# Weights in two and three pieces in place of four, and a new order of every queue, in an attention and feed-forward kernel

## The chip, the cores and the metric

The kernel runs on one core of one Trainium2 chip. The metric is the device time of one execution in microseconds; the time given is the median of three runs. The profile is of one more execution, taken by the hardware profiler.

## The reference

Linear attention over 8 batches and 8 heads (576 tokens, 64 dimensions), then a feed-forward part over the 4,608 tokens with 512 channels:

```
q_s = softmax(q, axis=-1);  k_s = softmax(k, axis=2)      # exp of (x - max), over its sum + 1e-9
kv  = einsum('bhsd,bhse->bhde', k_s, v)
x   = einsum('bhsd,bhde->bhse', q_s, kv)  ->  [4608, 512]
out = ((x @ w1) * (x @ w2)) @ w3 @ w_out                  # w1, w2: 512x1024; w3: 1024x1024; w_out: 1024x512
```

All inputs and the output are float32.

## The kernel before

Matrix work is done in fp16. w3 @ w_out is folded once into W3O (1024x512), so that each token needs two products up (with w2 and w1), an elementwise product, and one product down.

The tokens are worked in nine chunks of 512: chunk b (0 to 7) holds the first 512 tokens of batch b, and chunk 8 the last 64 of all eight. Chunks 0 and 1 are worked as two halves of 256 tokens (`sub` 0 and 1, four steps `u` each); the others as one piece (eight steps).

Every piece of work is a named step, and one list, ORDER, gives the order of all steps. Each engine runs its steps in the order of the list, so the list sets the order of every queue; what a step waits for follows from its data and its buffers. A suffix /A, /D or /P puts a step on ScalarE, VectorE or GpSimd. A step that uses the data path which VectorE and GpSimd share is linked to the one before it on the other engine. The steps, with the letters used below:

- loads: `w3.r` (a block of 128 rows of w3), `wo.h` (half of w_out), `w1.i` and `w2.i` (pieces by columns), `k.b`, `q.b`, `v.b` (a batch; some as two pieces, `k.0.0`, `q.1.1`). GpSimd issues those of the weights and of batches 0 and 1 (it casts the weights to fp16 on the way, line 302); SyncE issues q.0 at the start and all loads from batch 2 on. SyncE's first load after q.0 (`q.2`) is made to wait for the third-last load of GpSimd (GATE = 3).
- fold: `w3t.f` transposes a block of w3 on TensorE (L334), `w3T.f` evicts it (two buffers), `pf.f.0` and `pf.f.1` multiply it by w_out (L344), `W3O.f` evicts the result. `zero.i` are matmuls on zeros (L251), which fill TensorE's waits in the start; ZEROS gives 13 for `zero.0`, and for the others ORDER gives the count.
- attention of batch b: `kmx` (L375, L382), `cb` (the maximum over the tokens, spread to all partitions), `ksub` (L414), `kexp`; `qmx` (L477), `qsub` (L483), `qexp`, `qsm` (the sum, L509), `qeps`, `qrc`, `qn` (L527); `vc` (a cast of v, L220); `kv` on TensorE (L440), `kv2` divides by the sums (L458 to L461); `qd` transposes q by DMA (L561, on SyncE), for batch 0 `qt` and `qT` on TensorE and an eviction; `xm` and `xt` multiply q by kv (L579: the first 512 tokens and the last 64), `xs` and `xts` evict them (L224, L226).
- chunk c: `up.1.c.sub.u` multiplies by w2 and `up.0.c.sub.u` by w1 (L723, each into one PSUM bank of 512), `bs` evicts the first as fp16 (L220), `ab` multiplies the two (VectorE, L738), `down.c.t` multiplies 128 tokens by W3O (L745, L760 for the last chunk), `os` evicts them (L220), `st` stores them (SyncE).

TensorE writes into eight PSUM banks, taken in turn: a step waits until the bank taken eight places earlier has been evicted. GpSimd's loads have eight semaphores, also taken in turn, so that a load is issued only when the one eight places earlier has landed.

A step of `up` needs the piece of w1 or w2 that holds its columns; the piece is found from COLS:

```
COLS = [(0, 256), (256, 512), (512, 768), (768, 1024)]
ws = lambda n, u: [(n, [i for i, (a, b) in enumerate(COLS) if a < (u + 1) * nf * P <= b][0])]
```

Of the kernel before, what the change touches and what calls it, by code (L numbers as in the profile page):

```python
# [64 lines left out]
zero.6/1 zero.3/1 q.0.0 qmx.0.0 qsub.0.0/D q.0.1 qmx.0.1 ident w3.7 qexp.0.0 qsm.0.0 zero.1/6 zero.5/1 zero.0  # L65
w3.4 w3t.4 w3T.4/A qsub.0.1/D qexp.0.1 qeps.0.0/D qrc.0.0 qn.0.0/D w3t.7 w3T.7/A wo.0 zero.2/6 pf.4.0 qt.0.0.4
pf.7.0 qsm.0.1 qeps.0.1/D qrc.0.1 qt.0.0.0 w3.6 w3t.6 wo.1 pf.4.1 k.0.0 qn.0.1/D qT.0.0.4/A kmx.0.0 w3T.6/A
pf.7.1 W3O.7/A qT.0.0.0/A W3O.4/A k.0.1 kmx.0.1 cb.0 ksub.0.0/D qt.0.1.4 qt.0.1.0 pf.6.0 zero.4/1 w3.5 w3t.5
qT.0.1.0/A qT.0.1.4/A w3T.5/A pf.6.1 W3O.6/A w3.0 w3t.0 pf.5.0 pf.5.1 w3.3 w3T.0/A pf.0.0 w3t.3 pf.0.1 W3O.5/A
kexp.0.0 w3.2 w3t.2 w3.1 w3t.1 v.0 q.1.0 w2.3 w3T.3/D pf.3.0 pf.3.1 w3T.1/A ksub.0.1/D kexp.0.1 k.1 W3O.0/A  # L70
kv.0.0 qmx.1.0 kv.0 kv2.0 pf.1.0 pf.1.1 w2.2 w2.1 w3T.2/A W3O.3/A qsub.1.0/D xm.0.1 xm.0.0 xs.0.0.0/D
xs.0.1.0/D w1.2 q.1.1 w1.3 kmx.1.0 cb.1 pf.2.0 pf.2.1 w1.1 w2.0 w1.0 v.1 W3O.1/A xs.0.0.1/A up.1.0.0.3
xs.0.1.1/A qexp.1.0 up.1.0.1.3 up.1.0.1.2 bs.0.1.2/D qmx.1.1 ksub.1.0/P bs.0.0.3/A up.1.0.0.2 bs.0.1.3/A
up.1.0.0.1 up.1.0.1.1 bs.0.0.2/A W3O.2/A bs.0.0.1/A up.0.0.1.2 up.0.0.0.2 qsm.1.0 up.0.0.0.3 ab.0.0.3
bs.0.1.1/D ab.0.1.2 up.0.0.1.3 up.0.0.0.1 ab.0.1.3 ab.0.0.2 up.1.0.0.0 bs.0.0.0/D qeps.1.0/A qrc.1.0 ab.0.0.1
up.1.0.1.0 up.0.0.1.0 bs.0.1.0/A ab.0.1.0 qsub.1.1/P up.0.0.0.0 ab.0.0.0 qexp.1.1 qsm.1.1 kexp.1.0 up.0.0.1.1
ab.0.1.1 qeps.1.1/A qrc.1.1 ksub.1.1/P qn.1.0/P q.2 qmx.2.0 qmx.2.1 down.0.0 os.0.0/A kexp.1.1 down.0.1
os.0.1/A vc.1.0/P vc.1.1/P kv.1.0 kv.1 kv2.1 down.0.2 os.0.2/A k.2 kmx.2.0 kmx.2.1 xt.0 qd.1.0 xm.1.0 cb.2
qn.1.1/P down.0.3 st.0.0 xts.0.1/A qsub.2.0/P xs.1.0.0/A xts.0.0/A xs.1.0.1/A up.1.1.0.0 os.0.3/A up.0.1.0.0
up.1.1.0.1 bs.1.0.0/A ab.1.0.0 qd.1.1 qsub.2.1/P qexp.2.1 ksub.2.0/P qexp.2.0 qsm.2.0 xm.1.1 up.0.1.0.1  # L80
up.1.1.0.2 bs.1.0.1/A ab.1.0.1 xs.1.1.1/A up.0.1.0.2 up.1.1.0.3 xs.1.1.0/A kexp.2.0 qsm.2.1 qeps.2.0/A qrc.2.0
bs.1.0.3/A bs.1.0.2/A q.3 qmx.3.0 ksub.2.1/P qn.2.0/P up.0.1.0.3 ab.1.0.3 ab.1.0.2 up.1.1.1.0 up.0.1.1.0
up.1.1.1.1 bs.1.1.1/A qeps.2.1/A up.0.1.1.1 up.1.1.1.2 up.0.1.1.2 bs.1.1.0/A bs.1.1.2/A up.1.1.1.3 down.1.0
up.0.1.1.3 k.3 kmx.3.1 qrc.2.1 ab.1.1.1 qmx.3.1 ab.1.1.2 ab.1.1.0 v.2 q.4 qmx.4.1 vc.2.0/A qsub.3.0/P qexp.3.0
kexp.2.1 qd.2.0 qn.2.1/P st.0.1 down.1.1 os.1.0/A bs.1.1.3/A vc.2.1/P kv.2 os.1.1/A qsub.3.1/P qexp.3.1
ab.1.1.3 qsm.3.0 qeps.3.0/A down.1.2 os.1.2/A qd.2.1 kv2.2 xm.2.1 qsm.3.1 xs.2.1.1/A xm.2.0 xs.2.0.1/A xt.1
kmx.3.0 xs.2.0.0/A xs.2.1.0/A qsub.4.1/P down.1.3 qeps.3.1/A qrc.3.1 qn.3.1/P cb.3 ksub.3.1/P ksub.3.0/P
xts.1.1/A qexp.4.1 os.1.3/A xts.1.0/A qsm.4.1 qeps.4.1/A k.4 kmx.4.0 up.1.2.0.0 bs.2.0.0/A up.0.2.0.0
up.1.2.0.1 up.0.2.0.1 up.1.2.0.2 up.0.2.0.2 up.1.2.0.3 bs.2.0.2/A bs.2.0.1/A ab.2.0.0 ab.2.0.2 ab.2.0.1
qrc.4.1 qrc.3.0 up.0.2.0.3 bs.2.0.3/A ab.2.0.3 up.1.2.0.4 bs.2.0.4/A up.0.2.0.4 up.1.2.0.5 kexp.3.1 ab.2.0.4  # L90
qmx.4.0 up.0.2.0.5 up.1.2.0.6 v.3 st.1.1 q.5 up.0.2.0.6 up.1.2.0.7 up.0.2.0.7 vc.3.1/A bs.2.0.5/A kexp.3.0
bs.2.0.6/A vc.3.0/A kmx.4.1 ab.2.0.5 v.4 st.0.2 ab.2.0.6 qn.3.0/P st.1.2 qd.3.1 st.0.3 vc.4.1/P qn.4.1/P
qsub.4.0/P kv.3 bs.2.0.7/A ab.2.0.7 down.2.0 kv2.3 xt.2 xts.2.0/A os.2.0/A qd.3.0 cb.4 qmx.5.1 xm.3.1 xm.3.0
xs.3.0.1/D down.2.1 xts.2.1/A xs.3.1.1/A xs.3.1.0/A qexp.4.0 qsm.4.0 k.5 kmx.5.1 st.1.0 v.5 down.2.2 down.2.3
q.6 vc.4.0/A xs.3.0.0/A qeps.4.0/A qrc.4.0 os.2.1/A os.2.3/A up.1.3.0.0 up.0.3.0.0 bs.3.0.0/D qmx.5.0 ab.3.0.0
ksub.4.1/P kmx.5.0 cb.5 qsub.5.1/P qd.4.1 st.1.3 v.6 st.2.1 qn.4.0/P ksub.4.0/P up.1.3.0.1 up.0.3.0.1 os.2.2/A
bs.3.0.1/A qexp.5.1 kexp.4.1 up.1.3.0.2 up.0.3.0.2 up.1.3.0.3 up.0.3.0.3 up.1.3.0.4 up.0.3.0.4 bs.3.0.2/A
ab.3.0.1 ab.3.0.2 st.2.3 kexp.4.0 bs.3.0.3/A bs.3.0.4/A up.1.3.0.5 up.0.3.0.5 st.2.2 qsub.5.0/P ksub.5.1/P
vc.5.1/P up.1.3.0.6 up.0.3.0.6 up.1.3.0.7 ab.3.0.3 qsm.5.1 qmx.6.0 st.2.0 qd.4.0 ab.3.0.4 qexp.5.0 bs.3.0.6/A
bs.3.0.5/A ab.3.0.5 ab.3.0.6 kv.4 kv2.4 up.0.3.0.7 bs.3.0.7/A ab.3.0.7 qeps.5.1/A qsm.5.0 qeps.5.0/A down.3.0  # L100
os.3.0/A vc.5.0/A xm.4.0 xm.4.1 xt.3 down.3.1 down.3.2 xts.3.0/D qrc.5.0 xs.4.0.1/D qrc.5.1 qmx.6.1 ksub.5.0/P
qsub.6.0/P k.6 kmx.6.1 kmx.6.0 qsub.6.1/P xs.4.1.0/A os.3.1/A xs.4.0.0/A xs.4.1.1/A up.1.4.0.0 xts.3.1/D
vc.6.0/A down.3.3 qexp.6.0 qsm.6.0 os.3.3/A q.7 qmx.7.0 qn.5.1/P qn.5.0/P cb.6 ksub.6.0/P qsub.7.0/P kexp.5.1
kexp.5.0 os.3.2/A qd.5.0 k.7 st.3.1 qd.5.1 bs.4.0.0/A up.0.4.0.0 up.1.4.0.1 ab.4.0.0 v.7 bs.4.0.1/D up.0.4.0.1
up.1.4.0.2 up.0.4.0.2 bs.4.0.2/A qexp.6.1 up.1.4.0.3 up.0.4.0.3 bs.4.0.3/A up.1.4.0.4 up.0.4.0.4 ab.4.0.2
ab.4.0.1 qmx.7.1 ab.4.0.3 up.1.4.0.5 up.0.4.0.5 up.1.4.0.6 up.0.4.0.6 bs.4.0.6/D kv.5 bs.4.0.4/A kexp.6.0
bs.4.0.5/A ab.4.0.4 ab.4.0.5 ab.4.0.6 up.1.4.0.7 qeps.6.0/A qexp.7.0 qsm.7.0 up.0.4.0.7 bs.4.0.7/A ab.4.0.7
down.4.0 down.4.1 ksub.6.1/P kexp.6.1 st.3.3 st.3.0 qsm.6.1 kv2.5 qeps.7.0/A qrc.7.0 qeps.6.1/A qrc.6.1
os.4.1/D st.4.1 xt.4 qrc.6.0 xts.4.1/D os.4.0/A xts.4.0/A qsub.7.1/P qexp.7.1 vc.6.1/P kv.6 kv2.6 xm.5.1
qn.6.1/P xm.5.0 xs.5.0.1/A vc.7.1/A xs.5.0.0/A xs.5.1.1/A kmx.7.1 qsm.7.1 qeps.7.1/D st.3.2 down.4.2 down.4.3  # L110
os.4.3/D xs.5.1.0/A up.1.5.0.0 bs.5.0.0/A up.0.5.0.0 kmx.7.0 up.1.5.0.1 bs.5.0.1/A os.4.2/A up.0.5.0.1
up.1.5.0.2 up.0.5.0.2 up.1.5.0.3 ab.5.0.1 ab.5.0.0 qrc.7.1 up.0.5.0.3 up.1.5.0.4 up.0.5.0.4 up.1.5.0.5
up.0.5.0.5 qn.7.1/P bs.5.0.3/A bs.5.0.4/A cb.7 bs.5.0.2/D qn.6.0/D ab.5.0.2 ab.5.0.3 vc.7.0/P ksub.7.1/P
bs.5.0.5/A up.1.5.0.6 ab.5.0.4 bs.5.0.6/A up.0.5.0.6 ab.5.0.6 up.1.5.0.7 bs.5.0.7/A ab.5.0.5 qd.6.1 up.0.5.0.7
st.4.0 qd.6.0 st.4.2 ksub.7.0/D xm.6.0 xm.6.1 xt.5 qd.7.1 xs.6.0.1/A xs.6.0.0/A ab.5.0.7 down.5.0 down.5.1
os.5.1/D xs.6.1.1/D down.5.2 os.5.2/D kexp.7.1 os.5.0/D xts.5.0/A kexp.7.0 xts.5.1/A xs.6.1.0/A up.1.6.0.0
xt.6 xts.6.0/A qn.7.0/P qd.7.0 bs.6.0.0/A kv.7 kv2.7 up.0.6.0.0 ab.6.0.0 xts.6.1/D up.1.6.0.1 up.0.6.0.1
bs.6.0.1/A up.1.6.0.2 ab.6.0.1 bs.6.0.2/D st.4.3 xm.7.0 xm.7.1 xt.7 xts.7.0/A xs.7.1.1/A xs.7.0.1/A xts.7.1/D
xs.7.0.0/D up.0.6.0.2 up.1.6.0.3 xs.7.1.0/D st.5.2 st.5.1 bs.6.0.3/A ab.6.0.2 up.0.6.0.3 up.1.6.0.4 up.0.6.0.4
down.5.3 up.1.6.0.5 up.0.6.0.5 bs.6.0.4/A bs.6.0.5/A ab.6.0.4 ab.6.0.3 ab.6.0.5 os.5.3/D up.1.6.0.6 up.0.6.0.6  # L120
up.1.6.0.7 up.0.6.0.7 bs.6.0.6/A bs.6.0.7/A up.1.7.0.0 ab.6.0.6 up.0.7.0.0 ab.6.0.7 down.6.0 down.6.1 os.6.1/D
down.6.2 up.1.7.0.1 down.6.3 os.6.3/D bs.7.0.0/A os.6.2/A os.6.0/A up.0.7.0.1 ab.7.0.0 bs.7.0.1/D ab.7.0.1
up.1.7.0.2 bs.7.0.2/A up.0.7.0.2 up.1.7.0.3 ab.7.0.2 st.6.0 st.5.3 st.6.3 st.6.1 st.5.0 up.0.7.0.3 up.1.7.0.4
up.0.7.0.4 up.1.7.0.5 bs.7.0.4/A ab.7.0.4 bs.7.0.3/A ab.7.0.3 up.0.7.0.5 up.1.7.0.6 up.0.7.0.6 up.1.7.0.7
up.0.7.0.7 up.1.8.0.0 up.0.8.0.0 bs.7.0.6/D ab.7.0.6 bs.7.0.7/A bs.7.0.5/A ab.7.0.7 ab.7.0.5 bs.8.0.0/A
down.7.0 down.7.1 os.7.0/A st.7.0 down.7.2 up.1.8.0.1 bs.8.0.1/A ab.8.0.0 os.7.1/D st.7.1 up.0.8.0.1
up.1.8.0.2 up.0.8.0.2 up.1.8.0.3 up.0.8.0.3 ab.8.0.1 bs.8.0.3/D ab.8.0.3 os.7.2/A st.7.2 st.6.2 up.1.8.0.4
bs.8.0.4/D bs.8.0.2/D up.0.8.0.4 ab.8.0.2 up.1.8.0.5 up.0.8.0.5 bs.8.0.5/D ab.8.0.5 up.1.8.0.6 up.0.8.0.6
up.1.8.0.7 up.0.8.0.7 ab.8.0.4 bs.8.0.6/D ab.8.0.6 bs.8.0.7/D ab.8.0.7 down.8.0 os.8.0/A st.8.0 down.7.3
# [737 lines left out]
```

## Time and profile before

| | |
|---|---|
| median of 3 runs | 237.34 us (237.20 to 237.55) |
| the profiled execution | 237.48 us, span 235.7 us |
| TensorE busy | 229.4 us of the span |
| VectorE busy | 179.9 us |
| ScalarE, GpSimd busy | 118.8, 113.8 us |
| moved by DMA | 46.84 MB |

The span runs from the first to the last instruction that the profile shows; the time of an execution holds some 1.8 us more around it. A row of the timeline gives start and length in us, the engine, the line, the operation, out<-in, the shape and the count, and in brackets how long the engine had been idle before it and what ended that. A run of equal instructions is one row. A group row gives the total busy time and the mean in ns; a row of a load gives its size in SBUF and the us from issue to landing.

### The profile page before, as it was taken

The page shows a single profiled execution, that of the slowest core. Times are in us where ns is not written, and L with a number is a line of the kernel's source. Part 1 is how long each engine was busy: PE and PEld are TensorE (multiplying, and loading weights), DVE is VectorE, ACT ScalarE, POOL GpSimd, SP SyncE. Part 2 cuts the span into 40 slices and gives each one's busy share as a digit, 9 for nine tenths or more (in the row PEclk, how much of TensorE's full clock was granted, in tenths as well). Part 3 has the DMA queues.
Part 4 walks back from the last instruction along what each step waited for, and adds up shares of the span by engine and source line. Part 5 has one row for each costly group of instructions (what it writes and reads, how often), then busy time and mean ns, then how long its engine had stood idle before and what let it go on. Part 6 is the DMA issues. An engine that isn't in the chain of part 4 may idle for free.

```text
span 235.7 us, 4826 instructions
## 1 busy us (share of the span) xinstructions
PE 229.4 (97%) x1931; PEld 120.3 (51%) x1931; DVE 179.9 (76%) x299; ACT 118.8 (50%) x191; POOL 113.8 (48%) x77
## 2 busy tenths in 40 slices
...
GB/s 224 214 308 208 288 266 252 368 310 252 395 294 222 385 401 175 381 311 384 297 226 26 252 328 126 99 76 103 123 26 0 0 40 185 0 49 129 3 66 156
DMA packets 39798, 46.84 MB, mean 199 GB/s; under 512 B 18400, under 2 KB 23264, under 8 KB 39776
## 3 DMA queue, kind: packets, MB, share of 16 engines
...
q8 instruction: 15, 0.25, 0.4%
...
## 4 chain that ended last, share of the span: by engine, by line
PE 77%; DMA 12%; DVE 6%; POOL 2%; issue 2%; ACT 0%; DVEq 0%; POOLq 0%
PE pab L723 46%; PE po L745 23%; DMA k<-in_k_dram 6%; DMA w<-in_moe_w_dram 5%; PE po L760 3%; DVE ab L738 2%; PE pkv L440 2%; PE xm L579 1%; POOL w L302 1%; DVE bsb L220 1%; POOL k L302 1%; DVE qm L477 1%; DVE kmx L382 1%; POOL wosb L302 0%; PE xt L579 0%
## 5 line engine op out<-in xcount | busy, mean ns | idle before, releaser
L723 PE MATMUL pab<-x,w1sb 128*128 128x512 f16 (+1 forms) x320 | 64.9, 337 | 0.0
L723 PE MATMUL pab<-x,w2sb 128*128 128x512 f16 (+1 forms) x320 | 64.9, 336 | 0.0
L738 DVE TENSOR_TENSOR ab<-pab,bsb 128x512 f16<-128x512 f32 x72 | 46.8, 679 | 16.4 <-PE pab L723 15.9
L745 PE MATMUL po<-W3O,ab 128*128 128x512 f16 x256 | 58.8, 379 | 0.6 <-DVE ab L738 0.6
L220 ACT CAST bsb<-pab 128x512 f16<-128x512 f32 x56 | 32.0, 585 | 49.0 <-PE pab L723 45.6
L723 PEld LDWEIGHTS <-w2sb 128*128 128x128 f16 x352 | 34.4, 98 | 28.1
L723 PEld LDWEIGHTS <-w1sb 128*128 128x128 f16 x352 | 34.1, 98 | 27.7 <-issue 0.2
L414 POOL TENSOR_TENSOR k<-k,cb 128x1152 f32<-128x1152 f32 x13 | 34.1, 2626 | 11.4 <-DVE cb L410 8.3
L745 PEld LDWEIGHTS <-ab 128*128 128x128 f16 x256 | 24.2, 98 | 29.8 <-DVE ab L738 1.3
L527 POOL TENSOR_TENSOR en<-eq,qr 128x1280 f16<-128x1280 f16 (+1 forms) x13 | 27.8, 2140 | 12.6 <-DVE qr L520 11.2
L375 DVE TENSOR_REDUCE km<-k 128x128 f32<-128x1152 f32 x14 | 30.4, 2191 | 0.0
L220 ACT COPY osb<-po 128x512 f32<-128x512 f32 (+1 forms) x26 | 14.8, 577 | 30.7 <-PE po L760 15.9
L483 POOL TENSOR_TENSOR q<-q,qm 128x1280 f32<-128x1280 f32 (+1 forms) x13 | 27.8, 2143 | 3.6 <-DVE qm L477 3.6
L477 DVE TENSOR_REDUCE qm<-q 128x16 f32<-128x1024 f32 (+2 forms) x16 | 21.3, 1335 | 6.2 <-DMA q<-in_q_dram 6.2
L220 DVE COPY osb<-po 128x512 f32<-128x512 f32 (+1 forms) x11 | 7.2, 665 | 19.9 <-PE po L745 13.4
L509 DVE TENSOR_REDUCE qr<-eq 128x16 f32<-128x1024 f16 (+2 forms) x16 | 21.4, 1340 | 0.0
L491 ACT ACTIVATE eq<-q 128x1024 f16<-128x1024 f32 (+2 forms) x16 | 18.6, 1171 | 5.4 <-DVE q L483 5.3
L422 ACT ACTIVATE ek<-k 128x1152 f16<-128x1152 f32 x16 | 18.5, 1164 | 2.9 <-POOL k L414 1.9
L344 PE MATMUL pf<-wosb,w3T 128*128 128x512 f16 x64 | 15.5, 380 | 0.0
L224 ACT ACTIVATE x<-xm 128x512 f16<-128x512 f32 x25 | 13.9, 609 | 0.9 <-PE xm L579 0.9
L220 DVE CAST bsb<-pab 128x512 f16<-128x512 f32 x16 | 10.8, 680 | 4.3 <-PE pab L723 4.2
L251 PE MATMUL zero<-zero 128*128 128x512 f16 x29 | 9.5, 491 | 1.6 <-DVE zero L245 1.6
...
## 6 DMA issues: line engine op xcount, KB each, us to landing
...
q<-in_q_dram SPq DMA_DIRECT2D x6, 1152.0 KB, 10.0
k<-in_k_dram SPq DMA_DIRECT2D x6, 1152.0 KB, 7.2
v<-in_v_dram SPq DMA_DIRECT2D x6, 1152.0 KB, 9.4
w<-in_moe_w_dram POOLq DMA_DIRECT2D x8, 256.0 KB, 12.3
...
k<-in_k_dram POOLq DMA_DIRECT2D x1, 1152.0 KB, 14.9
```

Of the source, the lines that this page charges most:

```text
L220: return [(nc.scalar.copy if eng == "ACT" else engine[eng].tensor_copy)(out=out, in_=in_)]
L375: dve.tensor_reduce(out=st["km", b][:, two(hp), :], in_=kb[:, two(hp), :, :].rearrange("p h j d -> p h d j"), axis=AX.X, op=ALU.max)
L414: return [engine[eng].tensor_tensor(out=kb[:, two(hp), :, :], in0=kb[:, two(hp), :, :], in1=st["cb", b][:, two(hp), None, :].broadcast_to( ...
L422: nc.scalar.activation(out=st["ek", b][:, hp, :, :].rearrange("p j (i d) -> p i j d", i=2), in_=kb[:, two(hp), :, :], func=AF.Exp)
L477: dve.tensor_reduce(out=st["qm", b][:, hs, j], in_=qb[:, hs, j, :], axis=AX.X, op=ALU.max, **({"negate": True} if (b, p) in FEXP else {}))
L483: return [engine[eng].tensor_tensor(out=qb[:, hs, j, :], in0=qb[:, hs, j, :], in1=st["qm", b][:, hs, j, None].broadcast_to([P, nh, n, D]), ...
L491: nc.scalar.activation(out=st["eq", b, p], in_=qb[:, hs, j, :], func=AF.Exp)
L509: dve.tensor_reduce(out=st["qr", b][(slice(None), *part(p))], in_=st["eq", b, p], axis=AX.X, op=ALU.add)
L527: return [engine[eng].tensor_tensor(out=st["en", b][:, j, hs, :].rearrange("p j h d -> p h j d"), in0=st["eq", b, p], in1=st["qr", b][:, h ...
L723: nc.tensor.matmul(st["p", one, c, sub, u][:, a * (t1 - t0):(a + 1) * (t1 - t0)], lhsT=w[:, ct, fb * P:(fb + 1) * P], rhs=x()[:, ct, t0:t1 ...
L738: dve.tensor_tensor(out=st["ab", c][:, nf * u:nf * u + nf, t0:t1], in0=cut(st["p", 0, c, sub, u]), in1=cut(st["bsb", c, sub, u]), op=ALU.mult)
L745: nc.tensor.matmul(st["po", c, tb], lhsT=st["ab", c][:, ft, tb * P:(tb + 1) * P], rhs=W3O[:, ft, :], start=(ft == 0), stop=(ft == N_FT - 1))
```

## The change

w1 is loaded in two pieces of 512 columns, and w2 in pieces of 256, 256 and 512, where each had four pieces of 256. Steps 2 and 3 of w2 now wait for one piece, and so do steps 0 and 1, and 2 and 3, of w1. GpSimd issues 22 loads in place of 25.

The order of every queue is new. The zero matmuls are 26 in place of 29. Of the evictions and small steps some 80 change their engine, in both directions: VectorE has 214 steps in place of 203, ScalarE 178 in place of 189, GpSimd 69 in place of 72 (loads counted), TensorE and SyncE as many as before.

```diff
-    COLS = [(0, 256), (256, 512), (512, 768), (768, 1024)]
+    COLS = [(0, 256), (256, 512), (512, 1024)]
+    COLA = [(0, 512), (512, 1024)]
+    CUTS = {"w2": COLS, "w1": COLA}
...
-            cols = slice(*COLS[i])
+            cols = slice(*CUTS[n][i])
...
-    names += [(n, i) for n in ("w1", "w2") for i in range(len(COLS))]
+    names += [(n, i) for n in ("w1", "w2") for i in range(len(CUTS[n]))]
...
-        ws = lambda n, u: [(n, [i for i, (a, b) in enumerate(COLS) if a < (u + 1) * nf * P <= b][0])]
+        ws = lambda n, u: [(n, [i for i, (a, b) in enumerate(CUTS[n]) if a < (u + 1) * nf * P <= b][0])]
```

The list itself is rewritten from end to end. Taken apart by queue, these are the parts that the prediction speaks of (the steps of the queue named, in order; - is before, + after):

```diff
 GpSimd, the loads
-w3.7 w3.4 wo.0 w3.6 wo.1 k.0.0 k.0.1 w3.5 w3.0 w3.3 w3.2 w3.1 v.0 q.1.0 w2.3 k.1 w2.2 w2.1 w1.2 q.1.1 w1.3 w1.1 w2.0 w1.0 v.1
+w3.3 w3.4 wo.0 wo.1 w3.6 k.0.1 w3.0 k.0.0 w3.5 w3.7 w3.2 w3.1 v.0 k.1 w2.0 w2.1 q.1.0 w1.0 w2.2 q.1.1 w1.1 v.1
 GpSimd, behind the loads
-ksub.1.0 qsub.1.1 ksub.1.1 qn.1.0 vc.1.0 vc.1.1 qn.1.1
+ksub.1.0 qsub.1.1 qn.1.0 vc.1.1 vc.1.0 qn.1.1
 SyncE
-q.0.0 q.0.1 q.2 k.2 qd.1.0 st.0.0 qd.1.1 q.3 k.3 v.2 q.4 ...
+q.0.0 q.0.1 q.2 k.2 qd.1.0 v.2 qd.1.1 q.3 st.0.1 st.0.0 k.3 q.4 ...
 TensorE, the start and chunk 0
-zero.6 zero.3 zero.1 zero.5 zero.0 w3t.4 w3t.7 zero.2 pf.4.0 qt.0.0.4 pf.7.0 qt.0.0.0 w3t.6 pf.4.1 pf.7.1 qt.0.1.4 qt.0.1.0
-pf.6.0 zero.4 w3t.5 pf.6.1 w3t.0 pf.5.0 pf.5.1 pf.0.0 w3t.3 pf.0.1 w3t.2 w3t.1 pf.3.0 pf.3.1 kv.0.0 kv.0 pf.1.0 pf.1.1
-xm.0.1 xm.0.0 pf.2.0 pf.2.1 up.1.0.0.3 up.1.0.1.3 up.1.0.1.2 up.1.0.0.2 up.1.0.0.1 up.1.0.1.1 up.0.0.1.2 ...
+zero.0 zero.4 w3t.3 zero.3 w3t.4 zero.5 zero.1 pf.3.0 pf.4.0 pf.3.1 w3t.6 qt.0.0.4 qt.0.1.0 pf.4.1 qt.0.1.4 pf.6.0
+w3t.0 qt.0.0.0 pf.6.1 pf.0.0 w3t.5 pf.0.1 zero.6 w3t.7 w3t.2 pf.5.0 pf.7.0 pf.7.1 pf.5.1 w3t.1 kv.0.0 kv.0 pf.2.0 pf.2.1
+xm.0.0 xm.0.1 pf.1.0 pf.1.1 up.1.0.0.0 up.1.0.1.0 up.1.0.0.1 zero.2 up.1.0.1.1 up.0.0.0.0 up.0.0.0.1 up.0.0.1.1
+up.0.0.1.0 up.1.0.1.3 up.1.0.1.2 up.1.0.0.2 up.1.0.0.3 up.0.0.0.2 up.0.0.0.3 up.0.0.1.3 up.0.0.1.2 down.0.0 down.0.1 kv.1.0
 TensorE, the end of chunk 2, and of chunk 5
-kv.3 down.2.0 xt.2 xm.3.1 xm.3.0 down.2.1 ... xm.6.0 xm.6.1 xt.5 down.5.0 down.5.1
+kv.3 down.2.0 xm.3.1 xm.3.0 xt.2 down.2.1 ... down.5.0 xt.5 xm.6.0 kv.7 xm.6.1 xt.6 down.5.1
 VectorE, up to kv2.0
-... cb.0 ksub.0.0 w3T.3 ksub.0.1 qmx.1.0 kv2.0 qsub.1.0 xs.0.0.0 xs.0.1.0 kmx.1.0 cb.1
+... w3T.6 kmx.0.1 w3T.0 qT.0.1.0 kmx.0.0 cb.0 ksub.0.0 ksub.0.1 W3O.5 w3T.2 W3O.7 kv2.0 kmx.1.0 cb.1 qmx.1.0 bs.0.0.0 qsub.1.0 ksub.1.1
 VectorE, from kv2.2 to kv2.3
-kv2.2 qsm.3.1 kmx.3.0 qrc.3.1 cb.3 qsm.4.1 kmx.4.0 ab ab ab qrc.4.1 qrc.3.0 ab ab qmx.4.0 kmx.4.1 ab ab ab.2.0.7 kv2.3
+kv2.2 xts.1.1 qsm.3.0 kmx.3.0 qrc.3.0 cb.3 qsm.3.1 ab qrc.3.1 ab kmx.4.1 qsm.4.0 qmx.4.1 ab ab ab ab ab qmx.5.1 ab.2.0.7 kv2.3
 VectorE, the end of chunk 5
-... ab.5.0.5 ksub.7.0 ab.5.0.7
+... bs.5.0.7 ab.5.0.7
```

134 lines of the change are left out of this document (67 added, 67 removed).

## The prediction

> **What bounds the kernel now.** I read the page first (busy shares, the chain of waits), then windows of busy time, then TensorE's timeline for every pause it makes, and last the load issues.
>
> ```profile
> span 235.7 us, 4826 instructions
> PE 229.4 (97%) x1931; PEld 120.3 (51%) x1931; DVE 179.9 (76%) x299; ACT 118.8 (50%) x191; POOL 113.8 (48%) x77
> 56.00:76.00 20.00, 20.00 (x232) 15.34 (x231) 19.28 (x31) 14.80 (x23) 16.96 (x9) 1.00 1.03 305
> 76.00:95.00 19.00, 19.00 (x170) 8.81 (x169) 18.66 (x32) 13.52 (x25) 15.51 (x8) 1.00 1.09 321
> 142.00:165.00 23.00, 22.59 (x200) 10.30 (x189) 19.22 (x33) 13.03 (x22) 10.15 (x5) 1.00 0.47 97
> ```
>
> In the window rows the columns after the length are TensorE, its weight loads, VectorE, ScalarE, GpSimd, then the granted clock and the DMA share. TensorE never rests from 56 to 95 us; VectorE is busy for 37.9 of the same 39 us. TensorE sets the time, and VectorE runs so close behind it that an order which delays it by a microsecond can become the bound. The changed kernel does the same matmuls, so only three things can move the end: the number of filler matmuls, the pauses of the start, and the pauses after it.
>
> ```profile
> 1.55 7.63 PE L251 MATMUL zero<-zero 128*128 128x512 f16 x22 [1.55 <-DVE zero L245]
> 9.98 1.46 PE L251 MATMUL zero<-zero 128*128 128x512 f16 x6
> 18.56 0.71 PE L334 MATMUL w3t<-ident,w 128*128 128x128 f16 x8 [0.33 <-DMA w<-in_moe_w_dram]
> 24.41 1.13 PE L334 MATMUL w3t<-ident,w 128*128 128x128 f16 x16
> 33.22 5.40 PE L723 MATMUL pab<-x,w2sb 128*128 128x256 f16 x48
> 47.53 3.63 PE L745 MATMUL po<-W3O,ab 128*128 128x512 f16 x16 [0.17 <-DVE ab L738]
> 161.13 1.69 PE L745 MATMUL po<-W3O,ab 128*128 128x512 f16 x7
> 163.23 3.84 PE L745 MATMUL po<-W3O,ab 128*128 128x512 f16 x17 [0.41 <-DVE ab L738]
> 160.17 2.40 DVE L414 TENSOR_TENSOR k<-k,cb 128x1152 f32<-128x1152 f32 x1
> 162.49 0.68 DVE L738 TENSOR_TENSOR ab<-pab,bsb 128x512 f16<-128x512 f32 x1
> ```
>
> Up to 33.22 us TensorE folds w3 with w_out as the pieces arrive, and zero matmuls fill its waits. Then the first chunk's ups run without a break to 47.53. Later there is one pause worth naming: down.5.0 issues 7 matmuls from 161.13; at 0.216 us each (1.69 us is seven issue steps and the tail of the last) the eighth could have started at 162.64, and started at 163.23. It waited for ab.5.0.7 (162.49 + 0.68), which stood behind ksub.7.0 (2.40 us) on VectorE: a loss of 0.59.
>
> **The loads.** The wait in each row below is for the load eight places earlier, so the start of an issue dates that landing.
>
> ```profile
> 23.66 0.74 POOL L302 DMA_DIRECT2D w1sb<-in_moe_w_dram  x1 [1.56 <-DMA w<-in_moe_w_dram]
> 27.66 0.74 POOL L302 DMA_DIRECT2D w1sb<-in_moe_w_dram  x1 [2.15 <-DMA v<-in_v_dram]
> 33.99 0.74 POOL L302 DMA_DIRECT2D w1sb<-in_moe_w_dram  x1 [3.06 <-DMA k<-in_k_dram]
> 34.72 0.76 POOL L302 DMA_DIRECT2D v<-in_v_dram  x1
> w1sb<-in_moe_w_dram POOLq DMA_DIRECT2D x1, 256.0 KB, 9.9
> v<-in_v_dram POOLq DMA_DIRECT2D x1, 1152.0 KB, 12.3
> SPq L302 <- DMA w2sb<-in_moe_w_dram: 38.1, 1, 38.1
> 43.12 0.45 SPq L302 DMA_DIRECT2D k<-in_k_dram  x1
> 49.96 2.61 DVE L477 TENSOR_REDUCE qm<-q 128x16 f32<-128x1024 f32 x2 [0.32 <-DMA q<-in_q_dram]
> ```
>
> So w3.2 lands just before 23.66 and v.0 just before 27.66 (I take 23.5 and 27.5), w1.0 at 33.99 + 9.9 = 43.9, v.1 at 34.72 + 12.3 = 47.0. Between v.0 and w1.0 come 6,400 KB of fp32 source (a 256-column piece reads 512 KB, q.1 512 and 640, k.1 1,152): 16.4 us, or 390 KB/us. Up to w3.2, and again up to v.0, both kernels have asked for the same bytes (6,784 and 8,448 KB), so I keep both dates. After v.0 the new order at 390 KB/us lands k.1 at 30.5, w2.0 at 31.8, w2.1 at 33.1, q.1.0 at 34.4, w1.0 (512 columns) at 37.0, w2.2 (512) at 39.7, q.1.1 at 41.3, w1.1 at 43.9, v.1 at 46.9.
>
> **The change, part by part.** *Fillers.* 29 zero matmuls become 26, and only the one in the first chunk's ups (zero.2, 0.22 us) stands where TensorE has no wait to fill. The others lie ahead of the fold, which the loads pace; three fewer are worth nothing there.
>
> *Start.* With the new order TensorE reaches w3t.2 about 0.7 us before its block lands, so it goes on from 23.5. In the kernel before, w3t.2, w3t.1, three folds, kv.0 and xm.0 took 24.41 to 33.22, or 8.8 us with about 0.5 of waits and hand-overs. The new order has four folds behind that point; a fold is eight matmuls of 512 columns, 8 x 0.216 = 1.73. The first up then starts at 23.5 + 8.3 + 1.7, plus 0.3 for hand-overs = 33.8, against 33.22: 0.6 later (0.2 to 0.9).
>
> *Ups of the first chunk.* 128 half matmuls took 33.22 to 47.53 less the wait of 0.17, 14.14 us, 0.88 for a step of eight. In the new order up.0.0.0.0 is the fifth step, at 33.8 + 4 x 0.88 + 0.22 = 37.5, and needs w1.0 (37.0); the ninth needs w2.2 (39.7) at 41.1; the thirteenth, at 44.6, needs w1.1 (43.9). Each holds, with 0.5 to 1.4 us in hand. This is all that the larger pieces can do: fewer issues on GpSimd save nothing, since the transfers behind them and not the issue set the landings, and a whole 512 columns must be there before the first 256 can be used. Without that margin each 0.1 us of a late piece is 0.1 us of time. down.0.0 starts at 33.8 + 14.14 + 0.22 = 48.2, 0.6 after the kernel before.
>
> *VectorE in the start.* Six evictions move to VectorE ahead of kv2.0 (three w3T, two W3O, one qT), one w3T leaves, and the maximum over q.1.0 goes behind kv2.0.
>
> ```profile
> 28.78 1.22 DVE L477 TENSOR_REDUCE qm<-q 128x16 f32<-128x1024 f32 x1 [2.92 <-DMA q<-in_q_dram]
> L738 DVE TENSOR_TENSOR ab<-pab,bsb 128x512 f16<-128x512 f32 x72 | 46.8, 679 | 16.4 <-PE pab L723 15.9
> L375 DVE TENSOR_REDUCE km<-k 128x128 f32<-128x1152 f32 x14 | 30.4, 2191 | 0.0
> L509 DVE TENSOR_REDUCE qr<-eq 128x20 f32<-128x1280 f16 x7 | 10.3, 1470 | 0.0
> L509 DVE TENSOR_REDUCE qr<-eq 128x16 f32<-128x1024 f16 x7 | 8.4, 1206 | 0.0
> L477 DVE TENSOR_REDUCE qm<-q 128x20 f32<-128x1280 f32 x7 | 10.2, 1463 | 0.0
> ```
>
> At 0.68 an eviction that is some 3.4 - 1.2 = 2.2 us more before kv2.0, and the 2.92 us in which VectorE waited for q.1.0 hide it. Past kv2.0 it gains: k.1 lands at 30.5 and no longer at 33.7, so the maximum over k.1 starts three microseconds sooner.
>
> *The SyncE queue.* q.2 is held back by the third-last GpSimd load. That was w2.0 (SyncE waited 38.1 us for it, and k.2 followed at 43.12); it becomes q.1.1, at 41.3, so q.2 and k.2 are asked for while w1.1 and v.1 still load. In the trace v.1 landed 3.1 us after w1.0 (43.9 to 47.0, 370 KB/us) although q.2 stood in SyncE's queue, and q.2 landed at 49.96. I cost the earlier start at nothing, with the other bound below. The Trainium skill (DMA: Bandwidth & Descriptors, "Queues, rings and completion order") says that each DMA engine takes turns between the queues that have work, a packet at a time; by that rule v.1 should have run at half rate here, and the trace does not bear that out. Further down the queue, v.2 goes ahead of qd.1.1; it waits only for kv.0, long done, and delays nothing behind it.
>
> *After the start.* I went through each chunk's list, setting VectorE's steps against TensorE's. ab.5.0.7 now follows its bs at once, with no ksub in front: the pause of 0.59 goes, and next in line there is xm.6.0, whose inputs are microseconds old. The net of some ten steps more on VectorE falls mostly behind 142 us, where it idles (19.22 of 23 us). One place becomes tight:
>
> ```profile
> 75.52 0.49 DVE L461 TENSOR_TENSOR kv<-pkv,rc 128x128 f16<-128x128 f32 x2
> 94.23 0.49 DVE L461 TENSOR_TENSOR kv<-pkv,rc 128x128 f16<-128x128 f32 x2
> 95.32 0.25 PE L579 MATMUL xt<-qT,kv 64*64 64x64 f16 x8
> 95.61 0.63 PE L579 MATMUL xm<-qT,kv 64*64 64x512 f16 x8
> ```
>
> These are kv2.2 and kv2.3 on VectorE, then xt.2 and xm.3.1 on TensorE: kv2.3 is ready at 94.72, 0.89 before xm.3.1 uses it. Between the two kv2 the kernel before does three maxima over k, two wide q sums and a narrow q maximum (3 x 2.19 + 2 x 1.47 + 1.2 = 10.7); the new one does two, three q sums, two wide q maxima and an xtail (4.4 + 3.9 + 2.9 + 0.3 = 11.5), less one reciprocal of 0.25: 0.5 more. xt.2 (0.29 to the next start) moves behind xm.3. So 0.89 - 0.5 - 0.29 leaves 0.1 us. I charge nothing, and keep it as a rival.
>
> **The sum.** 0.6 from the start, less 0.59 from ab.5.0.7: 0.0. The profiled execution took 237.48 us (span 235.7 and 1.8 around it), 0.14 above the median of 237.34, so the forecast beside the median is **237.3 us**. About 0.2% (0.47 us) is what a measurement of this kernel can tell from no change; the forecast's own range, from the start's bounds of 0.2 and 0.9, with a little for hand-overs, is 236.9 to 237.8.
>
> **Rivals.** *Faster, by the start.* If w3.2 lands a microsecond sooner under the new order (w3.7 ahead of it), or the hand-overs vanish, the first up starts near 33.2 or before, and with the 0.59 the time is 237.34 - 0.6 = 236.7, at best 236.4. For it: the landing date is only as good as the wait of GpSimd. Against: v.0, kexp.0 and kv.0 come next, and v.0 is there no sooner than 27.5.
>
> *Slower, by VectorE at xm.3.1.* qmx.5.1 (1.46 us) now stands ahead of ab.2.0.7 and kv2.3. If VectorE is over 0.1 us later there than I count, TensorE waits: between 0 and 1.46, the middle 0.7, so 238.0. For it: VectorE is busy for 98% of that stretch. Against: it starts on k.1 three microseconds sooner.
>
> *Slower, by turns between queues.* q.2, issued at 41.3, takes half the rate from then on or from w1.1's end on. In the trace w1.0 still landed at 43.9, the full rate right behind q.2's issue, so I price the later bite: v.1 moves 1,152 KB at 195 KB/us, 5.9 us, and lands at 50.0 in place of 46.9. (From 41.3 on, w1.1 too would take 5.2 us in place of 2.6, to 46.5, 1.9 after its step is due: beyond the range, as no row shows the like.)
>
> ```profile
> 48.30 2.23 POOL L220 CAST v<-v 128x1152 f16<-128x1152 f32 x2
> ```
>
> The two casts of v.1 (1.14 us each, in the new order with qeps.1.1 on VectorE between them) then end at 52.6 and kv.1.0, due at 48.2 + 2 x 1.73 = 51.7, waits 0.9: 238.2. v.1's 3.1 us in the trace speak against it. This is what the rule of the Trainium skill named above would do here.
>
> **Chances.** The forecast 0.32; faster by the start 0.28; VectorE at xm.3.1 or a like place 0.26; the queues' turns 0.14. Faster by over 0.2%: 0.30, the second case and the forecast's lower edge. Within 0.2%: 0.30. Slower: 0.40. The range runs from the best of the faster case, 236.4, to both slow mechanisms together, 237.3 + 0.9 + 1.0 = 239.2.
>
> **What would show it.** The first 128x256 up at 33.5 to 34, with no wait for w1sb in it; the first po near 48.2; q issued on SyncE near 41.3 and v.1 still in near 47; no wait of seven-then-seventeen po matmuls near 161; xm.3.1 without idle time before it. A po near 47.5 or sooner, or a wait on kv before xm, shows the sum wrong, in that direction.

## The result and the profile after

The changed kernel takes 236.69 us (median of 20 runs, 236.46 to 237.23), the kernel before in the same session 237.28 (20 runs, 236.91 to 238.56). The ratio is 0.9977, 95% interval 0.9969 to 0.9985: 0.55 us or 0.23% faster, just past the 0.2% at which the prediction drew its line, with an interval of 0.15 to 0.31% that reaches to both sides of it. The forecast was 237.3, its own range 236.9 to 237.8, and the wide range 236.4 to 239.2.

The page and the chain of waits after:

```profile
span 234.9 us, 4814 instructions
PE 227.2 (97%) x1928; PEld 120.2 (51%) x1928; DVE 184.0 (78%) x310; ACT 114.7 (49%) x180; POOL 110.4 (47%) x74
PE 89%; DMA 9%; POOL 1%; issue 0%; ACT 0%; POOLq 0%; ACTq 0%
```

TensorE still sets the time: once w3.2 has landed, the whole chain is TensorE's. VectorE does 4.1 us more than before and delays nobody. TensorE's timeline at the places that the prediction named:

```profile
23.37 0.70 PE L336 MATMUL w3t<-ident,w 128*128 128x128 f16 x8 [0.52 <-DMA w<-in_moe_w_dram]
33.52 2.78 PE L725 MATMUL pab<-x,w2sb 128*128 128x256 f16 x24
36.14 0.38 PE L253 MATMUL zero<-zero 128*128 128x512 f16 x1
37.23 3.66 PE L725 MATMUL pab<-x,w1sb 128*128 128x256 f16 x32
40.73 3.66 PE L725 MATMUL pab<-x,w2sb 128*128 128x256 f16 x32
44.22 1.04 PE L725 MATMUL pab<-x,w1sb 128*128 128x256 f16 x8
47.71 3.62 PE L747 MATMUL po<-W3O,ab 128*128 128x512 f16 x16
53.80 0.26 PE L581 MATMUL xt<-qT,kv 64*64 64x64 f16 x8
53.88 0.39 PE L581 MATMUL xm<-qT,kv 64*64 64x256 f16 x8
54.21 1.90 PE L747 MATMUL po<-W3O,ab 128*128 128x512 f16 x8
95.41 0.63 PE L581 MATMUL xm<-qT,kv 64*64 64x512 f16 x8
95.87 0.23 PE L581 MATMUL xt<-qT,kv 64*64 64x64 f16 x8
96.03 5.35 PE L747 MATMUL po<-W3O,ab 128*128 128x512 f16 x24
160.32 1.89 PE L747 MATMUL po<-W3O,ab 128*128 128x512 f16 x8
224.63 7.09 PE L762 MATMUL po<-W3O,ab 128*128 128x512 f16 x40
```

From the first up at 33.52 to the end no row has a bracket, so TensorE waits for nothing that the profile names, and down.5.0 at 160.32 is eight matmuls in one piece. Rows of the kernel before that now matter, beside those that the prediction shows:

```profile
53.68 0.26 PE L579 MATMUL xt<-qT,kv 64*64 64x64 f16 x8
53.92 0.41 PE L579 MATMUL xm<-qT,kv 64*64 64x256 f16 x8
54.27 1.90 PE L745 MATMUL po<-W3O,ab 128*128 128x512 f16 x8
96.17 5.35 PE L745 MATMUL po<-W3O,ab 128*128 128x512 f16 x24
227.24 5.36 PE L760 MATMUL po<-W3O,ab 128*128 128x512 f16 x32
```

The first up starts 0.30 us later than before, the last matmul ends 0.88 sooner (231.72 against 232.60), so the stretch between them shrank from 199.38 to 198.20, by 1.18. Where: the pause at down.5.0, 0.59; the wait for an ab at the first po, gone; xt.0 to xm.1.0, 0.24 from start to start before and 0.08 now, 0.16; xt and xm of chunk 3, 95.32 to 96.17 before and 95.41 to 96.03 now, 0.23; less 0.22 for the filler at 36.14. The wait at the first po is 0.33: the bracket of 0.17 in its row starts at the end of the last up, but a next matmul could have started before that end. The last 24 half matmuls, 44.58 + 24 x 0.109, left room for the po at 47.20, and it started at 47.53. This is the way in which the pause at down.5.0 is 0.59 beside a bracket of 0.41.

That makes 1.09, and 0.09 is left over. All of it lies ahead of the po at 54: from there (54.27 before, 54.21 now) to the end the two traces differ by 0.82, which is the 0.59 and the 0.23. Counting in the timeline from the first up on, the 64-row matmuls (kv, xm, xt) stood in 14 separate runs between the wide ones and stand in 12 now; by this count two runs fewer gained nothing that shows.

The loads, by the issue row and its time to landing (issue of w1.0, w2.2, q.1.1, w1.1 and v.1 in this order):

```profile
w1sb<-in_moe_w_dram POOLq DMA_DIRECT2D x1, 512.0 KB, 15.7
w2sb<-in_moe_w_dram POOLq DMA_DIRECT2D x1, 512.0 KB, 16.0
q<-in_q_dram POOLq DMA_DIRECT2D x1, 640.0 KB, 16.5
w1sb<-in_moe_w_dram POOLq DMA_DIRECT2D x1, 512.0 KB, 16.0
30.71 0.75 POOL L304 DMA_DIRECT2D v<-in_v_dram  x1 [2.20 <-DMA k<-in_k_dram]
v<-in_v_dram POOLq DMA_DIRECT2D x1, 1152.0 KB, 16.8
```

Issued at 21.42, 23.61, 24.86, 27.77 and 30.71, they landed at 37.1, 39.6, 41.4, 43.8 and 47.5 (37.0, 39.7, 41.3, 43.9 and 46.9 in the prediction).

### The profile page after: what moved, and what is told of

Its sections match the earlier page's. It is cut to its first block, busy times and chain, and to the rows that moved or that the text cites. A ratio compares the mean times of both kernels' runs of the same rounds, so it can differ in the third digit from the quotient of the medians.

```text
span 234.9 us, 4814 instructions
## 1 busy us (share of the span) xinstructions
PE 227.2 (97%) x1928; PEld 120.2 (51%) x1928; DVE 184.0 (78%) x310; ACT 114.7 (49%) x180; POOL 110.4 (47%) x74
## 4 chain that ended last, share of the span: by engine, by line
PE 89%; DMA 9%; POOL 1%; issue 0%; ACT 0%; POOLq 0%; ACTq 0%
PE pab L725 53%; PE po L747 24%; DMA w<-in_moe_w_dram 5%; DMA wosb<-in_moe_w_out_dram 3%; PE pf L346 3%; PE po L762 3%; PE pkv L442 2%; PE xm L581 2%; POOL w L304 1%; PE w3t L336 1%; PE xt L581 0%; PE pkv L451 0%; ACT osb L222 0%; POOL ident masks.py:199 0%; PE zero L253 0%
## 5 line engine op out<-in xcount | busy, mean ns | idle before, releaser
L740 DVE TENSOR_TENSOR ab<-pab,bsb 128x512 f16<-128x512 f32 x72 | 47.6, 681 | 15.7 <-PE pab L725 14.6
L222 ACT CAST bsb<-pab 128x512 f16<-128x512 f32 x54 | 31.0, 585 | 47.7 <-PE pab L725 43.1
L416 POOL TENSOR_TENSOR k<-k,cb 128x1152 f32<-128x1152 f32 x12 | 31.5, 2628 | 14.2 <-DVE k L416 8.3
L222 ACT COPY osb<-po 128x512 f32<-128x512 f32 (+1 forms) x28 | 15.9, 579 | 42.8 <-PE po L747 30.9
L222 DVE CAST bsb<-pab 128x512 f16<-128x512 f32 x18 | 12.3, 683 | 16.3 <-PE pab L725 16.2
L226 ACT ACTIVATE x<-xm 128x512 f16<-128x512 f32 x25 | 13.2, 606 | 1.4 <-PE xm L581 1.4
L222 DVE COPY osb<-po 128x512 f32<-128x512 f32 (+1 forms) x9 | 5.9, 654 | 6.7 <-PE po L747 2.8
L346 PEld LDWEIGHTS <-w3T 128*128 128x128 f16 x64 | 5.7, 98 | 8.0 <-ACT w3T L222 2.3
```

What stands on the lines that cost most here:

```text
L222: return [(nc.scalar.copy if eng == "ACT" else engine[eng].tensor_copy)(out=out, in_=in_)]
L346: nc.tensor.matmul(st["pf", ft], lhsT=st["w3T", ft][:, gt, :], rhs=wosb[:, gt, :], start=(gt == 0), stop=(gt == N_FT - 1))
L416: return [engine[eng].tensor_tensor(out=kb[:, two(hp), :, :], in0=kb[:, two(hp), :, :], in1=st["cb", b][:, two(hp), None, :].broadcast_to( ...
L740: dve.tensor_tensor(out=st["ab", c][:, nf * u:nf * u + nf, t0:t1], in0=cut(st["p", 0, c, sub, u]), in1=cut(st["bsb", c, sub, u]), op=ALU.mult)
```

## Experiments

Theory A was that the larger pieces are worth nothing, and that the gain is the pause and the other places above, fewer runs of 64-row matmuls among them. Each run was timed in five rounds beside the kernel before; the changed kernel stands at 0.9977. "Stretch" is the time from the first up to the end of the last matmul in the profiled execution.

| run | median us (before) | ratio, 95% interval | first up | stretch |
|---|---|---|---|---|
| before | 237.28 | 1 | 33.22 | 199.38 |
| changed | 236.69 (237.28) | 0.9977, 0.9969 to 0.9985 | 33.52 | 198.20 |
| e1 four pieces | 237.07 (237.47) | 0.9978, 0.9967 to 0.9990 | 34.02 | 198.19 |
| e2 pause alone | 236.74 (237.47) | 0.9964, 0.9949 to 0.9980 | 33.93 | 198.59 |
| e3 pause back | 237.62 (237.47) | 1.0009, 0.9994 to 1.0024 | 33.78 | 198.89 |
| e4 filler moved | 236.62 (237.47) | 0.9962, 0.9949 to 0.9974 | 34.47 | 197.80 |
| e5 old start | 236.75 (237.45) | 0.9968, 0.9956 to 0.9981 | 33.70 | 198.35 |
| e6 new start | 237.41 (237.45) | 0.9999, 0.9989 to 1.0009 | 33.41 | 198.96 |
| e7 runs split | 237.66 (237.45) | 1.0006, 0.9994 to 1.0017 | 33.24 | 198.98 |
| e8 late kv2.3 | 238.34 (237.45) | 1.0045, 1.0032 to 1.0059 | 33.25 | 200.08 |
| e9 pieces in the old order | 239.06 (237.36) | 1.0069, 1.0050 to 1.0087 | 34.03 | 200.68 |
| e10 early q.2 | 243.90 (237.36) | 1.0251, 1.0223 to 1.0279 | 33.45 | 205.60 |
| e11 fold first | 237.72 (237.36) | 1.0018, 1.0001 to 1.0035 | 34.47 | 198.17 |
| e12 no filler | 236.71 (237.36) | 0.9969, 0.9957 to 0.9982 | 33.98 | 198.30 |

The two columns at the right have to be read apart. With the same order up to it, the first up comes anywhere from 33.24 to 34.02 in the eight traces with the new start (changed, e1, e3, e6, e7, e8, e10, e12), and from 33.22 to 34.03 in the four with the start of the kernel before (before, e2, e5, e9). So one profile says little about a start, and the 33.22 that the prediction started from is the earliest of its kind. (e4 and e11 change the start itself; in e4, besides, TensorE waited 1.07 us for a block of w3.) The stretch tells smaller differences, but single waits of 0.1 to 0.6 us come and go in it too.

**e1, four pieces.** COLS of four for both weights; the order reads "w1.0 w1.1", "w2.2 w2.3" and "w1.2 w1.3" where it read w1.0, w2.2 and w1.1; GATE = 4.

> The changed kernel with both weights in four pieces of 256 columns again; each larger piece's two halves are loaded one after the other at its place, and the load of q.2 waits for the same piece of q.1. Theory A (the gain is the pause of 0.59 us at down.5.0, a wait of 0.17 for an ab, a wait of about 0.2 for a landing of the transposed q near 95 us, and fewer changes between wide and 64-row matmuls; the pieces are worth nothing): 236.7 us as the changed kernel, within 0.2, first up at 33.5, no wait for a weight in the ups. Rival B (the two issues fewer on GpSimd bring the gain): back to 237.3.

The same ratio as the changed kernel and the same stretch, and no wait for a weight. Three loads fewer are worth nothing that these runs show; the two intervals leave room for some 0.3 us either way.

**e2, the pause alone.** In the order of the kernel before:

```
- st.4.2 ksub.7.0/D xm.6.0 xm.6.1 xt.5 qd.7.1 xs.6.0.1/A xs.6.0.0/A ab.5.0.7 down.5.0
+ st.4.2 xm.6.0 xm.6.1 xt.5 qd.7.1 xs.6.0.1/A xs.6.0.0/A ab.5.0.7 ksub.7.0/D down.5.0
```

> The kernel before with one step moved: the subtraction ksub.7.0 goes on VectorE from ahead of ab.5.0.7 to behind it. Theory A: the 0.59 us between the seventh and the eighth po matmul of down.5.0 goes and nothing takes its place, so 236.7 us. Rival C (the gain comes from the new start and hand-overs, and the pause is refilled by the next wait, for xm or kv): 237.1 to 237.3.

TensorE's row at down.5.0 in this run, where the kernel before had 7 and 17 (down.5.0 to down.5.2 in one row now):

```profile
161.63 5.35 PE L745 MATMUL po<-W3O,ab 128*128 128x512 f16 x24
```

One step moved gives 0.85 us (0.47 to 1.20), all of what the whole change gives or more. The profiled stretch is 0.79 shorter, more than the 0.59, because two waits of the kernel before were smaller or absent in this execution, whose first up came at 33.93: 0.08 in place of 0.33 at the first po, and none at xm.3.1; others were longer.

**e3, the pause back.** In the order of the changed kernel, qsm.7.0 from behind kv2.7 to ahead of ab.5.0.7.

> The changed kernel with one step moved: the sum qsm.7.0 (VectorE, 1.2 us) goes from behind kv2.7 to just ahead of ab.5.0.7. Theory A: ab.5.0.7 ends 1.2 us later, at 162.9, the eighth po matmul of down.5.0 is due at 161.83, so a pause of 1.1 to 1.2 and 237.8 us. Rival C (a later ab is absorbed further on, as TensorE isn't what ends the time there): 236.7.

VectorE's rows (bs.5.0.7, qsm.7.0, ab.5.0.7) and TensorE's:

```profile
160.37 0.63 DVE L222 CAST bsb<-pab 128x512 f16<-128x512 f32 x1
160.92 1.20 DVE L511 TENSOR_REDUCE qr<-eq 128x16 f32<-128x1024 f16 x1
162.04 0.68 DVE L740 TENSOR_TENSOR ab<-pab,bsb 128x512 f16<-128x512 f32 x1
160.39 1.67 PE L747 MATMUL po<-W3O,ab 128*128 128x512 f16 x7
162.78 0.39 PE L747 MATMUL po<-W3O,ab 128*128 128x512 f16 x1 [0.71 <-DVE ab L740]
```

The eighth matmul could have started at 160.39 + 7 x 0.216 = 161.90 and started 0.88 later, not 1.1 to 1.2, because qsm.7.0 first filled a gap of VectorE. The time went up by 0.0032 of 237.45, 0.76 us, the stretch by 0.69: nearly all of such a pause reaches the end. Rival C is out.

**e4 and e12, the filler.** e4 moves zero.2 from the ups to ahead of w3t.2; e12 leaves it out (25 fillers).

> The changed kernel with its one filler matmul of the first chunk's ups (zero.2) moved ahead of w3t.2, where TensorE waits 0.52 us for a block of w3. Theory A: the filler's 0.22 us goes from the path and lies in the wait, so 236.5 us, with the first up at 33.5 as before. Rival (the clock or a bank depends on the filler): 236.7 or more.

> The changed kernel without the one filler in the first chunk's ups (zero.2), the six others as they are. Theory A: the ups follow each other without the 0.22 us, first up as before, 236.5 us. Rival (a filler there costs nothing): 236.7.

The 128 half matmuls of the ups and the filler took 33.52 to 47.71, 14.19 us; without it 13.98 (e4) and 13.97 (e12). By the time e4 gains 0.36 and e12 0.19 on the changed kernel, neither clear of its interval, but 0.22 is what the timeline shows. e12's stretch is no shorter than that of the changed kernel, as it met a wait that most of the others escape:

```profile
90.84 1.93 SPq L563 DMA_TRANSPOSE qT<-en  x1
96.21 0.63 PE L581 MATMUL xm<-qT,kv 64*64 64x512 f16 x8 [0.51 <-PE po L747]
```

The bracket names a po that had been done; kv2.3 had ended at 95.39. The transposed q (qd.3.1), issued at 90.84 behind six stores on SyncE, lands some 5 us later (4.8 in the changed kernel, 5.3 here): 96.1, and xm.3.1 starts at 96.21. In the changed kernel it lands at 90.28 + 4.8 = 95.1, 0.3 before use; in the kernel before at 89.89 + 5.6 = 95.5, and xm.3.1 started at 95.61. That explains the 0.23 of chunk 3, but as a wait of one execution and not of the order: e2, whose queues are those of the kernel before there, has no such wait, and neither have e6 and e9.

```profile
95.90 0.26 PE L579 MATMUL xt<-qT,kv 64*64 64x64 f16 x8
95.99 0.61 PE L579 MATMUL xm<-qT,kv 64*64 64x512 f16 x8
```

These are xt.2 and xm.3.1 of e2, 0.09 apart where the profile of the kernel before has 0.29. With the new order the wait is absent in the changed kernel and there in e12.

**e5 and e6, the two halves exchanged.** e5 is the kernel before up to down.0.0 and the changed order from there; e6 the reverse.

> The kernel before up to down.0.0 (its order, its pieces, its 29 fillers), and from there on the order of the changed kernel. Theory A (the changed start costs some 0.3 to 0.5 us with its filler, the rest of the order gains 1.2): first up at 33.2 as in the kernel before, the rest as in the changed kernel, 236.1 to 236.3 us, under both kernels. Rival D (the new start is worth something): 236.7 or more.

> The other way round: the changed kernel with its pieces up to down.0.0, and from there on the order of the kernel before. Theory A: the pause of 0.59 us near 161 us is back, and so are the changes between wide and 64-row matmuls, so 237.6 to 237.9 us. Rival D (start and pieces gain): under 237.3.

e6 is level with the kernel before (within 0.24 us either way): the new start with its pieces and its filler costs nothing net, and gains nothing that shows. e5 gains 0.76 (0.45 to 1.04): the gain lies behind the first chunk, and it is no more than e2 has from the pause alone. But e5 was expected 0.5 lower. Its first up came at 33.70 and not at 33.2, and it met a wait that the changed kernel has not:

```profile
53.85 0.26 PE L579 MATMUL xt<-qT,kv 64*64 64x64 f16 x8
54.33 0.41 PE L579 MATMUL xm<-qT,kv 64*64 64x256 f16 x8 [0.23 <-DMA qT<-en]
```

xm.1.0 follows xt.0 by 0.48 where the changed kernel needs 0.08, since it waits for the transposed q.

**e7, runs split.** In the order of the changed kernel:

```
- xm.6.0 xs.6.0.0/D xs.6.0.1/A qn.7.1/P kv.7 xm.6.1 xt.6 kv2.7 qsm.7.0 down.5.1 down.5.2 down.5.3
+ xm.6.0 xs.6.0.0/D xs.6.0.1/A qn.7.1/P down.5.1 kv.7 xm.6.1 kv2.7 qsm.7.0 down.5.2 xt.6 down.5.3
```

> The changed kernel with its one run of 64-row matmuls in chunk 5 (xt.5, xm.6.0, kv.7, xm.6.1, xt.6) cut in three by down.5.1 and down.5.2 between them; no matmul more or fewer. Theory A (each run of 64-row matmuls costs 0.09 us going in and 0.08 us coming out): two runs more cost 0.3 us, 237.0 us. Rival E (the order of matmuls of other shapes costs nothing): 236.7.

Dearer than expected: 0.69 by the time, 0.78 by the stretch. From xt.5 to the end of down.5.3 it took 161.79 to 168.84, 7.05 us, against 162.14 to 168.66, 6.52: 0.26 for each of the two runs more. The other 0.24 is a wait of xm.7.0 for its transposed q. This is the price of these two cuts. It does not carry over to the whole change: two runs fewer should then have gained 0.5, and behind 54 us nothing is left over for them. What stands in a run, and in which order, counts too: near 75 us kv, xm and xt stand in two runs in both kernels, and from the start of a run to the next wide matmul the two took 1.34 us before and take 1.49 now.

**e8, kv2.3 late.** kmx.4.0 from behind xts.2.1 to ahead of down.2.0 and kv2.3.

> The changed kernel with the maximum kmx.4.0 (VectorE, 2.2 us) moved ahead of kv2.3, which the trace shows ready 0.24 us before xm.3.1 uses it. Theory A (the margin is what the trace shows, and nothing later takes it up, as TensorE sets the time): kv2.3 comes 2.2 later, xm.3.1 waits 1.9 to 2.0, 238.6 us. Rival F (the landing of the transposed q sets xm.3.1, or the wait is made good later): 236.7 to 237.2.

```profile
94.07 2.16 DVE L376 TENSOR_REDUCE km<-k 128x128 f32<-128x1152 f32 x1
96.61 0.49 DVE L462 TENSOR_TENSOR kv<-pkv,rc 128x128 f16<-128x128 f32 x2
96.96 0.82 PE L580 MATMUL xm<-qT,kv 64*64 64x512 f16 x8 [1.62 <-DVE kv L462]
```

kv2.3 came 1.93 later (96.61 against 94.68), xm.3.1 waited 1.62, and the time rose by 0.0068, 1.6 us. The margin was 0.3 us, and what exceeds it is paid in full. (Expected were a wait of 1.9 to 2.0 and 238.6.)

**e9, the larger pieces in the order of the kernel before.**

```
- ... q.1.0 w2.3 ... w2.2 w2.1 ... w1.2 q.1.1 w1.3 ... w1.1 w2.0 w1.0 v.1
+ ... q.1.0 w2.2 ... w2.1 w2.0 ... w1.1 q.1.1 ...      w1.0 v.1
```

> The kernel before in its own order, with the larger pieces of the changed kernel: w2.2 and w2.1 stay pieces of 256 columns, w2.1 and w2.0 of the kernel before become one piece of 512 at the place of the first, w1.2 and w1.3 one at the place of the first, w1.1 and w1.0 likewise; q.2 waits for q.1.1. Theory A (a piece of 512 is worth nothing where it lands ahead of its first use, and costs its lateness where it doesn't): at 390 KB/us the pieces land at 37.0, 39.7 and 43.9 us and are due at 36.7, 38.8 and 43.2, so waits of 0.3, 0.9 and 0.7 before the ups and 239.2 us. Rival B (fewer and larger loads gain by themselves): 237.3 or less.

```profile
40.01 3.67 PE L725 MATMUL pab<-x,w1sb 128*128 128x256 f16 x32 [0.58 <-DMA w1sb<-in_moe_w_dram]
44.17 1.05 PE L725 MATMUL pab<-x,w1sb 128*128 128x256 f16 x8 [0.49 <-DMA w1sb<-in_moe_w_dram]
```

1.6 us slower (239.06, expected 239.2): the first chunk took 34.03 to 49.84, 15.81 against 14.31, with the waits at the two pieces of w1. The wait expected at w2 did not come. The pieces alone, in an order that doesn't suit them, cost; it is the new order of the first chunk that keeps them free of charge.

**e10, q.2 early.** GATE = 6 in the changed kernel.

> The changed kernel with q.2 on SyncE held back by the load of q.1.0 (landing near 35 us) in place of that of q.1.1 (41.3), so q.2 and k.2, 2,304 KB together, are asked for six microseconds sooner, while w1.0, w2.2, q.1.1, w1.1 and v.1 load. Theory A (the loads of GpSimd's queue keep their rate, as v.1 did in the kernel before): 236.7 us, no wait for a weight in the ups. Rival G (the queues take turns): w1.0 lands about 1.3 us after it is due and w2.2 some 3 after, 239 to 240 us.

```profile
49.13 6.12 PE L725 MATMUL pab<-x,w1sb 128*128 128x256 f16 x32 [4.46 <-DMA w1sb<-in_moe_w_dram]
w2sb<-in_moe_w_dram POOLq DMA_DIRECT2D x1, 512.0 KB, 17.4
w1sb<-in_moe_w_dram POOLq DMA_DIRECT2D x1, 512.0 KB, 21.6
```

Theory A failed here: 243.9 us where it expected 236.7. With q.2 and k.2 asked for at 34.9 and 35.4, w1.0 still landed at 37.2, but w2.2 at 23.51 + 17.4 = 40.9 (1.3 later than in the changed kernel) and w1.1 at 27.52 + 21.6 = 49.1 (5.3 later). VectorE began on q.1.1 at 43.46, on its landing; from there w1.1's 1,024 KB of source took some 5.7 us, 180 KB/us, less than half of 390. Rival G is right in kind, though not in the amount (239 to 240): w1.0, landing 2.3 us after q.2 was issued, was not delayed, and w1.1 was hit hardest. Why the first one escaped is not shown. The price is more than the wait of 4.46: the clock dropped too (last section).

**e11, fold first.** In the changed order w3T.3 and w3T.4 ahead of qexp.0.1.

> The changed kernel with the two first w3T copies on ScalarE moved ahead of qexp.0.1, so that TensorE's wait of 1.44 us for w3T.3 at 11.9 us goes. Theory A (the landing of w3.2 sets the start: in every run with this start the first up follows w3t.2 by 10.1 to 10.2 us): TensorE waits longer at w3t.2, the first up still comes 10.15 us after it, 236.7 us. Rival H (TensorE's own work sets the start): first up up to 0.5 us sooner, 236.2.

```profile
17.33 0.40 PE L554 MATMUL qtp<-ident,en 128*128 128x128 f16 x4 [0.99 <-DVE en L529]
23.58 1.12 PE L336 MATMUL w3t<-ident,w 128*128 128x128 f16 x16
29.62 0.48 PE L442 MATMUL pkv<-v,ek 64*64 64x64 f16 x36 [0.26 <-ACT ek L424]
```

Both wrong: 1.0 us slower than the changed kernel (1.0018 against 0.9977). The exponential that was put back delayed the softmax of q.0, TensorE waited for that instead, and w3t.7 and w3t.2 now run without a wait for w3.2, half a microsecond after it could have started. The start has two limits, the loads and the softmax of q.0, close behind each other in this run.

The best version that was run is e4, 0.9962; its interval meets that of the changed kernel.

## Why the prediction was right or wrong

**The bound and the loads: right.** Landings within 0.1 us up to w1.1, and no wait in the ups. The margins were thinner than reckoned: w1.0 landed at 37.1 and was used at 37.23, where 0.5 was expected.

**Pieces: right** that they are worth nothing where they land in time (e1), and that a late one costs its lateness (e9).

**Fillers: right.** Only zero.2 counts, 0.21.

**The start: its step right, its worth wrong.** 10 us of work from w3t.2 to the first up plus 0.3 of hand-overs were predicted; it is 10.15 in the changed kernel and 10.10 to 10.17 in e3, e4, e6, e7, e8 and e12. The first up came at 33.52 (33.8 predicted), 0.30 behind the profile of the kernel before, at the lower end of 0.2 to 0.9. But the sum charged 0.6 for the start, at the first up and again at down.0.0, and e6 measured 0.0 net, within 0.24. Three things were missed. The first up varies by 0.8 from one execution to the next, so that 33.22 was no firm date to be late against. The ups take 13.97 and not 14.14, since the wait at the first po was 0.33 and not the 0.17 of its bracket. And xm.1.0 waited 0.16 for its transposed q, a wait that the new start does not have. In the traces these waits belong to the old start: at the first po 0.33 (before) and 0.08 (e2, e5), at xm.1.0 0.16, 0.23 and 0.40 (the same three), while none of the eight traces with the new start has either. That they are what pays for the filler and for a later first up is read from these traces; no run tested it by itself.

**The pause: right.** e2 and e3 show it from both sides. Nothing took its place.

**VectorE: right in the forecast, not in the margin.** kmx.1.0 started at 30.45, as soon as kv2.0 was done. For xm.3.1 the prediction left 0.1 us behind kv2.3; e8 shows 0.3. The difference is the 0.29 that it took off for xt.2: xt.2 needs 0.09 (e2), and the rest was a wait for a second input of xm.3.1 that the prediction never looked at, the transposed q, which lands no earlier (e12).

**SyncE's queue: right result, wrong reason.** q.2 was issued when q.1.1 landed, near 41.4, and v.1 landed at 47.5, 0.6 later than predicted; kv.1.0 at 51.26 did not wait. The prediction held that the kernel before spoke against turns between the queues. The rule of the Trainium skill (DMA: Bandwidth & Descriptors, "Queues, rings and completion order"), that an engine takes turns between the queues that have work, fits e10, where w1.1 ran at 180 KB/us. In the changed kernel q.2 was issued at 41.4, with only w1.1 (landing at 43.8) and v.1 still to come; so it is the date that spared it, and no right of way of GpSimd's loads.

**The sum: the step that failed.** It had two terms, +0.6 from the start and -0.59 from the pause, and came to 0. The second is right. The first was too large: e6 puts it at 0.0, within 0.24. By the traces, the 0.6 that was still to be paid behind the first chunk is -0.06 at the po of 54 us (54.21 against 54.27): the first up came 0.28 sooner than forecast, the ups were 0.17 shorter, and xm.1.0's wait of 0.16 went. With the start at nothing the sum is the pause alone, -0.59, and 0.55 to 0.59 was measured; 0.59 also lies within the intervals of e2 and e5, which lack the pause and keep the old start.

The two profiled executions differ by more, 0.82 us (237.48 and 236.66), mostly because that of the kernel before was 0.20 above its median: +0.30 for the first up, -0.59, -0.33, -0.16, -0.23, -0.09 and +0.22 make -0.88 for the end of the last matmul. Of these the -0.23 at xm.3.1 is a chance of that execution, as e2, e6 and e9 show.

So the time fell outside the forecast's own range, 236.9 to 237.8, and within the wide one, at the number of the rival "faster, by the start" (236.7). That the rival's number fits is luck: its mechanism did not occur, as w3.2 landed at 23.3 us in the changed kernel and at 23.4 before, and the first up was not early. The start just cost nothing.
